# Spreading a weight conversion over two experts and moving token steps in a fused scan, mixture and gated-layer kernel

## The chip, the cores and the metric

The kernel runs on one core of a Trainium2 chip. The metric is device microseconds of one execution; before the change the median of three runs is 889.12 us (888.71 to 890.1). One more execution was profiled: it took 889.29 us, and its span from the first to the last instruction is 887.6 us. PE is the matrix engine (TensorE), DVE the vector engine, ACT the scalar engine, POOL is GpSimd, and SP issues the DMAs. Times inside the profile are microseconds from the start of the span.

## The reference, cut to what matters

Three layers follow each other on 3072 tokens of width 256. The first is a decayed scan over 4 sequences of 8 heads. Its result goes through four weighted experts, and their sum through a gated layer:

```python
x = scan(x, a, B, C)                       # (3072, 256)
p = domain_probs / (domain_probs.sum(-1, keepdims=True) + 1e-09)
out = 0
for e in range(4):                         # w1[e]: 256 x 1024, w2[e]: 1024 x 256
    h = np.maximum(x @ w1[e], 0.0)
    out += p[:, e:e + 1] * (h @ w2[e])
g = out @ w_gate                           # 256 x 1536
silu = g * (1.0 / (1.0 + np.exp(-g)))
val = out @ w_val
return silu * val @ w_out                  # 1536 x 256
```

The weights of the gated layer (called the dense layer below) are handed to the kernel as 64-bit numbers, which it turns into 32-bit ones itself.

## The kernel before, in words

Each operand of a matrix product is split into a high part (rounded to the matrix engine's fp32r) and a low part (the rest), and each product is three matmuls: high by high, low by high, high by low. A matmul takes 128 x 128 weights against 512 tokens.

The program text sets the order on every engine; the engines run in order and wait for one another by semaphores. The text has three stages:

- Scan together with experts 0 and 1, up to about 327 us.
- Experts 2 and 3. A unit is (expert, block of 512 tokens, chunk of 128 hidden columns): 2 x 6 x 8 = 96 units. `m_hidden` multiplies into a PSUM bank; ACT makes the high part `hh` (L551), DVE the low part `hl` (L552). `m_out`, three units later (LAG = 3), multiplies by the second weights into `po`. At the end of a block DVE multiplies by the token's probability (`tmp`, L572) and adds into `acc` (L574). Each unit has two slots at which other work is written in, so there are 192 slots.
- The dense layer in 18 quads: 3 pairs of token blocks by 6 quads of hidden columns. A quad has two halves: the gate (`what` = 0) and the value (`what` = 1). A half is seven products, after a scheme with seven instead of eight block products, in four PSUM banks X, Y, Z, W. The first four open the banks (A11, S2, S1, S3), then `rest` adds three more onto X, Z and W. ACT copies X to `c1` (tile `c`) before the fifth product may add onto X; DVE adds it up to `u` and `v`. In the gate's half ACT applies the silu to four results `s` (one straight from X, three after a DVE addition); in the value's half DVE multiplies the values with them, ACT makes the high part `ah` (L830) and POOL the low part `al` (L832). The two parts of four results (keys 22, 11, 12, 21) are multiplied by the output weights one quad later, in `dense_project`, between the products. The last quad's low parts are all made by DVE.

Two kinds of preparation run beside this. `dense_chunk` converts the dense weights in nine chunks (gate, value and output for each of three groups of columns). A chunk has two loads, two runs of nine DVE steps (L624 to L644), for gate and value four sums on POOL (`ws`, L658), then high parts on ACT (`wd_h`, L673), low parts on POOL (`wd_l`, L675) and two stores to DRAM. Chunks 3 to 8 are stored only and loaded again; chunks 0 to 2 also stay resident for the first pair. `dense_steps` strings the steps of several chunks into one list, and `spread` puts the list evenly over a range of the 192 slots. Before, the six chunks 3 to 8 lie in slots 18 to 96 and the three chunks 0 to 2 in slots 102 to 188 (n1 = 96 is where expert 3 begins).

`dense_tokens` prepares a pair of token blocks for the seven-product scheme in six steps s0 to s5: high parts on ACT (`xh`, `t3h`, `t24h`, L732), low parts and differences on POOL (L735, L738). For the first pair the steps lie in expert 3's slots 136 to 178, as they do after the change. For the other pairs they were written behind a quad: s0 and s1 behind the first quad of the pair before, s2, s3, s4 and s5 behind the second to fifth.

Of the kernel before, what the change touches and what calls it, by code (L numbers as in the profile page):

```python
# [16 lines left out]
def kernel(ctx: ExitStack, tc: tile.TileContext, nat_d, bc_d, bc0_d, a_d, probs, w1, w2, wg, wv, wo, out):  # L17
# [12 lines left out]
    nc = tc.nc  # L30
# [9 lines left out]
    KD = DM // P  # L40
    FC1 = F1 // P
# [6 lines left out]
    LAG = 3  # L48
# [21 lines left out]
    bxh = [xpool.tile([P, KD, BN], F32R, name=f"xh{i}", tag=f"xh{i}") for i in range(NBLK)]  # L70
    bxl = [xpool.tile([P, KD, BN], F32R, name=f"xl{i}", tag=f"xl{i}") for i in range(NBLK)]
    bacc = [xpool.tile([P, KD, BN], F32, name=f"acc{i}", tag=f"acc{i}") for i in range(NBLK)]
# [264 lines left out]
    def a_diff(q):  # L337
        L = Q[q]["L"]
        nc.vector.tensor_tensor(out=L, in0=L, in1=cols(cum, q).unsqueeze(2).to_broadcast([P, H, P]), op=ALU.subtract)
# [187 lines left out]
    def bank(pool, tag):  # L527
        return pool.tile([P, 512], F32, tag=tag, name=tag)
# [162 lines left out]
    def dense_steps(chunks):  # L691


        parts = [dense_chunk(*c) for c in chunks]
        seq = list(parts[0][0])
        stores = []
        for i, (_, halves, splits, own) in enumerate(parts):
            ahead = parts[i + 1][0] if i + 1 < len(parts) else [None, None]
            for z in range(2):
                seq += halves[z]  # L700
                if ahead[z]:
                    seq.append(ahead[z])
                if z == 0:
                    seq += stores
            seq += splits
            stores = own
        return seq + [lambda: None] * 8 + stores
# [17 lines left out]
    xt = {}  # L725

    def dense_tokens(p):

        b1, b2 = 2 * p, 2 * p + 1
        G = nc.gpsimd  # L730
        def high(out, raw):
            nc.scalar.activation(out=out, in_=raw, func=AF.Copy)  # L732

        def low(out, raw, hi):
            G.tensor_tensor(out=out, in0=raw, in1=hi.bitcast(F32), op=ALU.subtract)  # L735

        def sub(out, a, b):
            G.tensor_tensor(out=out, in0=a, in1=b, op=ALU.subtract)  # L738

        def s0():  # L740
            high(bxh[b1], bacc[b1])
            high(bxh[b2][:, 1, :], bacc[b2][:, 1, :])
            low(bxl[b2][:, 1, :], bacc[b2][:, 1, :], bxh[b2][:, 1, :])

        def s1():

            sub(bacc[b2][:, 1, :], bacc[b2][:, 1, :], bacc[b2][:, 0, :])
            low(bxl[b1], bacc[b1], bxh[b1])

        def s2():  # L750

            sub(bacc[b2][:, 0, :], bacc[b2][:, 0, :], bacc[b1][:, 0, :])
            G.tensor_tensor(out=bacc[b1][:, 0, :], in0=bacc[b2][:, 1, :], in1=bacc[b1][:, 0, :], op=ALU.add)

        def s3():

            sub(bacc[b1][:, 1, :], bacc[b1][:, 1, :], bacc[b1][:, 0, :])
            xt[p, "t3"] = [dpools["xt"].tile([P, BN], F32R, tag=f"t3{z}", name=f"t3{z}", bufs=2) for z in "hl"]
            high(xt[p, "t3"][0], bacc[b2][:, 1, :])
            high(bxh[b2][:, 0, :], bacc[b2][:, 0, :])  # L760
            low(bxl[b2][:, 0, :], bacc[b2][:, 0, :], bxh[b2][:, 0, :])

        def s4():
            xt[p, "t24"] = [dpools["xt"].tile([P, KD, BN], F32R, tag="xt", name=f"t24{z}") for z in "hl"]
            high(xt[p, "t24"][0], bacc[b1])
            low(xt[p, "t3"][1], bacc[b2][:, 1, :], xt[p, "t3"][0])

        def s5():
            low(xt[p, "t24"][1], bacc[b1], xt[p, "t24"][0])

        return [s0, s1, s2, s3, s4, s5]


    A11, A22, A12, S1, S2, S3, S4 = range(7)

    def operand(p, name):
        b1, b2 = 2 * p, 2 * p + 1
        if name == "T3":
            return xt[p, "t3"]
        v, k = {  # L780
            "B11": ((bxh[b1], bxl[b1]), 0),
            "B21": ((bxh[b1], bxl[b1]), 1),
            "B22": ((bxh[b2], bxl[b2]), 1),
            "T1": ((bxh[b2], bxl[b2]), 0),
            "T2": (xt.get((p, "t24")), 0),
            "T4": (xt.get((p, "t24")), 1),
        }[name]
        return [z[:, k, :] for z in v]

    def product(ps, w, a, v, start):  # L790
        ws = slice(a * P, (a + 1) * P)
        (wh, wl), (vh, vl) = w, v
        for i, (x, y) in enumerate([(wh, vh), (wl, vh), (wh, vl)]):
            nc.tensor.matmul(ps, x[:, ws], y, start=(start and i == 0), stop=(i == 2), skip_group_check=True)  # L794

    def temp(tag):
        if tag in ("c1", "u"):
            return mpool.tile([P, BN], F32, tag="ma" if tag == "c1" else "mb", name=tag)
        return dpools["dt"].tile([P, BN], F32, tag=tag, name=tag, bufs=5 if tag == "s" else 1)

    def dense_hidden(p, q, what, s):

        w = wq.pop((p, q, what))
        X, Y, Z, W = (bank(*b) for b in (banks[0], banks[1], banks[2], banks[3]))
        V = nc.vector
        put = lambda ps, a, v, start: product(ps, w, a, operand(p, v), start)
        c1, u, v = temp("c1"), temp("u"), temp("v")
        put(X, A11, "B11", True)
        nc.scalar.activation(out=c1, in_=X, func=AF.Copy)
        put(Y, S2, "T2", True)  # L810
        V.tensor_tensor(out=u, in0=Y, in1=c1, op=ALU.add)  # L811
        put(Z, S1, "T1", True)
        V.tensor_tensor(out=v, in0=Z, in1=u, op=ALU.add)  # L813
        put(W, S3, "T3", True)

        def out(key, ps, add, dst):

            if what == 0:
                s[key] = temp("s")
                if add is not None:  # L820
                    V.tensor_tensor(out=s[key], in0=ps, in1=add, op=ALU.add)  # L821
                nc.scalar.activation(out=s[key], in_=ps if add is None else s[key], func=AF.Silu)  # L822
                return
            if add is not None:
                V.tensor_tensor(out=dst, in0=ps, in1=add, op=ALU.add)
            av = s.pop(key)
            V.tensor_tensor(out=av, in0=ps if add is None else dst, in1=av, op=ALU.mult)  # L827
            ah = hpool.tile([P, 512], F32R, tag="hh", name="ah")
            al = hpool.tile([P, 512], F32R, tag="hl", name="al")
            nc.scalar.activation(out=ah, in_=av, func=AF.Copy)  # L830
            low = V if (p, q) == quads[-1] else nc.gpsimd
            low.tensor_tensor(out=al, in0=av, in1=ah.bitcast(F32), op=ALU.subtract)  # L832
            hid[p, q, key] = ah, al

        out(22, W, v, v)

        def rest():
            put(X, A12, "B21", False)
            out(11, X, None, None)
            put(Z, S4, "B22", False)  # L840
            out(12, Z, u, v)
            put(W, A22, "T4", False)
            out(21, W, u, u)
        return rest
# [27 lines left out]
    with tc.manual_schedule():  # L872
# [20 lines left out]
        def add(u, half, fn):  # L893
            todo.setdefault((u, half), []).append(fn)
# [5 lines left out]
        for q in range(NFIRST, NQ):  # L900
            for o, fn in points(q).items():
                if q == NFIRST and o < -4:
                    fn = {-7: lambda: a_diff(2), -6: lambda: a_causal(2)}.get(o)
                elif q == NFIRST and o == -4:
                    fn = lambda: a_weigh_b(2, nc.gpsimd)
# [27 lines left out]
        def spread(seq, slots):  # L933
            for i, fn in enumerate(seq):
                add(*slots[i * len(slots) // len(seq)], fn)
# [2 lines left out]
        add((2, 0, 0), 0, opens)  # L938
        slots = [(u, h) for u in units23 for h in range(2)]
        n1 = len(slots) // 2  # L940
        spread(dense_steps([(c, False) for c in (3, 4, 5, 6, 7, 8)]), slots[2 * (8 + LAG) - 4:n1])
        spread(dense_steps([(c, True) for c in (0, 1, 2)]), slots[n1 + 2 * LAG:-4])
        n2 = n1 + 2 * (2 * FC1 + LAG) + 2
        spread(dense_tokens(0), slots[n2:n2 + 42])

# [12 lines left out]
        quads = [(p, q) for p in range(NPAIR) for q in range(NQD)]  # L958
        AHEAD = 2
        dtodo = {}  # L960
# [7 lines left out]
        def project_part(i):  # L968
            if before:
                dense_project(*before, parts[i], outw[before])  # L970
            elif i < 2:
                for u in units[-LAG:-1] if i == 0 else units[-1:]:
                    m_out(u)
# [3 lines left out]
        for i, (p, q) in enumerate(quads):  # L977
            if i + AHEAD < len(quads):
                dense_load(*quads[i + AHEAD])
            outw[p, q] = wq.pop((p, q, 2))  # L980
            s = {}
            for what in range(2):
                rest = dense_hidden(p, q, what, s)
                project_part(2 * what)
                rest()
                project_part(2 * what + 1)
            for fn in dtodo.pop((p, q), []):
                fn()
            before = p, q
        for i in range(4):  # L990
            project_part(i)
# [53 lines left out]
```

## Time and profile before

| what | value |
| --- | --- |
| median of three runs | 889.12 us (888.71 to 890.1) |
| the profiled execution | 889.29 us, span 887.6 us |
| PE busy | 865.8 us, 98% of the span |
| DVE, ACT, POOL busy | 577.6, 343.8, 323.0 us |
| mean granted clock of PE | 0.989 |

Shares of the whole span hide the stages. The views to read are PE's timeline (when does a matmul start later than the pace of its neighbours), the table by windows, what the late ones waited for, and the chain of waits.

### The profile page before, as it was taken

The page shows a single profiled execution, that of the slowest core. Times are in us where ns is not written, and L with a number is a line of the kernel's source. Part 1 is how long each engine was busy: PE and PEld are TensorE (multiplying, and loading weights), DVE is VectorE, ACT ScalarE, POOL GpSimd, SP SyncE. Part 2 cuts the span into 40 slices and gives each one's busy share as a digit, 9 for nine tenths or more (in the row PEclk, how much of TensorE's full clock was granted, in tenths as well). Part 3 has the DMA queues.
Part 4 walks back from the last instruction along what each step waited for, and adds up shares of the span by engine and source line. Part 5 has one row for each costly group of instructions (what it writes and reads, how often), then busy time and mean ns, then how long its engine had stood idle before and what let it go on. Part 6 is the DMA issues. An engine that isn't in the chain of part 4 may idle for free.

```text
span 887.6 us, 12199 instructions
## 1 busy us (share of the span) xinstructions
PE 865.8 (98%) x4484; PEld 713.0 (80%) x4484; DVE 577.6 (65%) x884; ACT 343.8 (39%) x598; POOL 323.0 (36%) x276
## 2 busy tenths in 40 slices
PE   9999999999999999999899999998999999999997
PEld 8888888888888888887678888886877877788885
DVE  6877566656654443789776666736666766667675
ACT  5555444444343332222222233224344443444432
POOL 6755333323331121331330154204464374625250
PEclk8999999999999999999999999999999999999999
DMA  7844433343250132144352223034344264537301
GB/s 219 284 144 138 137 113 114 119 134 116 94 163 13 38 114 63 60 142 164 135 199 83 72 108 127 23 134 161 128 141 156 92 245 141 172 107 261 107 1 47
DMA packets 45523, 111.12 MB, mean 125 GB/s; under 512 B 5016, under 2 KB 12376, under 8 KB 45464
## 3 DMA queue, kind: packets, MB, share of 16 engines
q1 hardware_dynamic: 45464, 110.35, 36.8%
q8 instruction: 35, 0.57, 0.2%
q14 instruction: 24, 0.20, 0.1%
HBM read 92.88 MB, written 17.45 MB: 124 GB/s over the span
## 4 chain that ended last, share of the span: by engine, by line
PE 78%; DVE 11%; ACT 3%; issue 3%; POOL 2%; DMA 1%; SPq 0%; ACTq 0%; DVEq 0%; POOLq 0%
PE h L508 21%; PE po L516 18%; PE h L794 12%; PE po L861 5%; PE d L794 5%; PE d L516 5%; PE d L861 4%; PE d L508 2%; DVE hl L552 2%; PE ypsum L437 1%; POOL ws L658 1%; PE scores L391 1%; PE ypsum L400 1%; DVE dr L630 1%; DVE dr L634 1%
## 5 line engine op out<-in xcount | busy, mean ns | idle before, releaser
L552 DVE SCALAR_TENSOR_TENSOR hl<-h,hh 128x512 fp32r<-128x512 f32 (+1 forms) x184 | 117.9, 642 | 175.8 <-ACT hh L551 175.7
L551 ACT ACTIVATE hh<-h 128x512 fp32r<-128x512 f32 (+1 forms) x184 | 102.0, 560 | 267.5 <-PE h L508 267.5
L832 POOL TENSOR_TENSOR al<-s,ah 128x512 fp32r<-128x512 f32 x68 | 100.5, 1507 | 157.0 <-ACT ah L830 142.3
L508 PE MATMUL h<-xh,w_h 128*128 128x512 f32 (+1 forms) x368 | 139.0, 378 | 0.6 <-DVE hl L552 0.4
L508 PE MATMUL h<-xl,w_h 128*128 128x512 f32 (+1 forms) x368 | 137.5, 374 | 0.5 <-DVE xl L476 0.5
L508 PE MATMUL h<-xh,w_l 128*128 128x512 f32 (+1 forms) x368 | 137.0, 372 | 0.4 <-POOL w_l L125 0.4
L516 PE MATMUL po<-hh,w_l 128*128 128x512 f32 (+1 forms) x320 | 118.0, 369 | 2.1 <-POOL w_l L125 2.1
L516 PE MATMUL po<-hl,w_h 128*128 128x512 f32 (+1 forms) x320 | 118.1, 369 | 1.5 <-DVE hl L552 1.5
L516 PE MATMUL po<-hh,w_h 128*128 128x512 f32 (+1 forms) x320 | 118.5, 370 | 1.1 <-ACT L L349 0.6
L830 ACT ACTIVATE ah<-s 128x512 fp32r<-128x512 f32 x72 | 45.3, 632 | 101.8 <-DVE s L827 86.5
L508 PEld LDWEIGHTS h<-xh,w_h 128*128 128x128 f32 x368 | 69.4, 189 | 16.2 <-issue 3.6
L508 PEld LDWEIGHTS h<-xl,w_h 128*128 128x128 f32 x368 | 69.5, 189 | 14.5 <-DVE xl L476 2.6
L508 PEld LDWEIGHTS h<-xh,w_l 128*128 128x128 f32 x368 | 69.4, 189 | 11.9 <-POOL w_l L125 0.6
L516 PEld LDWEIGHTS po<-hl,w_h 128*128 128x128 f32 x320 | 60.3, 188 | 12.4 <-DVE hl L552 2.3
L516 PEld LDWEIGHTS po<-hh,w_h 128*128 128x128 f32 x320 | 60.3, 188 | 12.0 <-issue 1.3
L516 PEld LDWEIGHTS po<-hh,w_l 128*128 128x128 f32 x320 | 60.2, 188 | 12.0 <-POOL w_l L125 2.3
L811 DVE TENSOR_TENSOR u<-h,c 128x512 f32<-128x512 f32 x36 | 24.9, 692 | 62.0 <-PE h L794 36.4
L358 POOL TENSOR_TENSOR Bs<-bc,Bs 64x512 fp32r<-64x512 f32 x22 | 31.3, 1421 | 81.4 <-issue 72.0
L794 PE MATMUL h<-xh,wq_h 128*128 128x512 f32 x128 | 50.5, 394 | 2.1 <-DVE v L813 2.0
L822 ACT ACTIVATE s<-s 128x512 f32<-128x512 f32 x54 | 34.1, 631 | 46.0 <-DVE s L821 45.3
L658 POOL TENSOR_TENSOR ws<-dr 128x256 f32<-128x256 f32 x12 | 9.0, 753 | 114.4 <-DVE dr L644 114.4
L794 PE MATMUL h<-xl,wq_h 128*128 128x512 f32 x128 | 49.8, 389 | 0.0
(221 smaller groups left out, 1775.4 us busy)
## 6 DMA issues: line engine op xcount, KB each, us to landing
wq_h<-wd_d SPq DMA_DIRECT2D x32, 448.0 KB
wq_l<-wd_d SPq DMA_DIRECT2D x32, 448.0 KB
bc<-in_bc_dram SPq DMA_DIRECT2D x22, 512.0 KB
L<-crow_d SPq DMA_DIRECT2D x22, 512.0 KB
wq_o<-wo_d SPq DMA_DIRECT2D x16, 512.0 KB
nat<-in_nat_dram SPq DMA_DIRECT2D x24, 256.0 KB
raw<-in_w_dram SPq DMA_DIRECT2D x11, 512.0 KB
pbc<-probs_d SPq DMA_DIRECT2D x22, 256.0 KB
```

Of the source, the lines that this page charges most:

```text
L358: nc.gpsimd.tensor_tensor(out=r["Bs"][64:], in0=r["Br"][64:], in1=r["Bs"][64:].bitcast(F32), op=ALU.subtract)
L508: nc.tensor.matmul(ps, w[:, k, fs], v[:, k, :], start=(i == 0), stop=(i == len(ops) - 1))
L516: nc.tensor.matmul(po[d], w[:, fc, dsl], x, start=(first and i == 0), stop=(last and i == 2))
L551: nc.scalar.activation(out=hh, in_=ph, func=AF.Relu)
L552: nc.vector.scalar_tensor_tensor(out=hl, in0=ph, scalar=0.0, in1=hh.bitcast(F32), op0=ALU.max, op1=ALU.subtract)
L658: nc.gpsimd.tensor_tensor(out=v[:, :, o, :], in0=a, in1=b, op=op)
L794: nc.tensor.matmul(ps, x[:, ws], y, start=(start and i == 0), stop=(i == 2), skip_group_check=True)
L811: V.tensor_tensor(out=u, in0=Y, in1=c1, op=ALU.add)
L822: nc.scalar.activation(out=s[key], in_=ps if add is None else s[key], func=AF.Silu)
L830: nc.scalar.activation(out=ah, in_=av, func=AF.Copy)
L832: low.tensor_tensor(out=al, in0=av, in1=ah.bitcast(F32), op=ALU.subtract)
L861: nc.tensor.matmul(po[d], x[:, dsl], y, start=(first and i == 0), stop=(last and i == 2))
```

## The change

Three edits. The nine chunks' steps are spread anew: chunks 3 to 8 over slots 8 to 128 and chunks 0 to 2 over slots 128 to 188. The token steps of the next pair are written behind the gate's first four products of the same quads, no longer behind the quad; two high parts of 1024 columns are split in two of 512. In the last quad the low parts of keys 22 and 11 go to POOL; those of 12 and 21 stay on DVE.

```diff
         def s0():
-            high(bxh[b1], bacc[b1])
+            for k in range(KD):
+                high(bxh[b1][:, k, :], bacc[b1][:, k, :])
             high(bxh[b2][:, 1, :], bacc[b2][:, 1, :])
             low(bxl[b2][:, 1, :], bacc[b2][:, 1, :], bxh[b2][:, 1, :])
...
         def s4():
             xt[p, "t24"] = [dpools["xt"].tile([P, KD, BN], F32R, tag="xt", name=f"t24{z}") for z in "hl"]
-            high(xt[p, "t24"][0], bacc[b1])
+            for k in range(KD):
+                high(xt[p, "t24"][0][:, k, :], bacc[b1][:, k, :])
             low(xt[p, "t3"][1], bacc[b2][:, 1, :], xt[p, "t3"][0])
...
-            low = V if (p, q) == quads[-1] else nc.gpsimd
+            low = V if (p, q) == quads[-1] and key in (12, 21) else nc.gpsimd
             low.tensor_tensor(out=al, in0=av, in1=ah.bitcast(F32), op=ALU.subtract)
...
-        spread(dense_steps([(c, False) for c in (3, 4, 5, 6, 7, 8)]), slots[2 * (8 + LAG) - 4:n1])
-        spread(dense_steps([(c, True) for c in (0, 1, 2)]), slots[n1 + 2 * LAG:-4])
+        cut = n1 + 4 * FC1
+        spread(dense_steps([(c, False) for c in (3, 4, 5, 6, 7, 8)]), slots[FC1:cut])
+        spread(dense_steps([(c, True) for c in (0, 1, 2)]), slots[cut:-4])
...
                 rest = dense_hidden(p, q, what, s)
+                if what == 0:
+                    for fn in dtodo.pop((p, q), []):
+                        fn()
                 project_part(2 * what)
                 rest()
                 project_part(2 * what + 1)
-            for fn in dtodo.pop((p, q), []):
-                fn()
             before = p, q
```

How the instructions stand on the engines, at three places. On DVE in expert 2, one run of nine conversion steps of chunk 4 (tile f) among the low parts hl of the units; before:

```order
L552 SCALAR_TENSOR_TENSOR hl<-d_3793,hh 128x512
L624 TENSOR_SCALAR dr<-f_3715 128x2x256
L626 TENSOR_SCALAR dr<-dr 128x2x256
L628 TENSOR_SCALAR dr<-dr 128x2x256
L552 SCALAR_TENSOR_TENSOR hl<-h_3820,hh 128x512
L630 SCALAR_TENSOR_TENSOR dr<-f_3715,dr 128x2x256
L632 TENSOR_SCALAR f_3715<-f_3715 128x512
L634 TENSOR_TENSOR dr<-dr,f_3715 128x2x256
L636 TENSOR_SCALAR f_3715<-f_3715 128x512
L552 SCALAR_TENSOR_TENSOR hl<-h_3841,hh 128x512
```

and now, the same run of steps:

```order
L552 SCALAR_TENSOR_TENSOR hl<-h_3784,hh 128x512
L626 TENSOR_SCALAR dr<-dr 128x2x256
L628 TENSOR_SCALAR dr<-dr 128x2x256
L630 SCALAR_TENSOR_TENSOR dr<-f_3650,dr 128x2x256
L552 SCALAR_TENSOR_TENSOR hl<-d_3804,hh 128x512
L632 TENSOR_SCALAR f_3650<-f_3650 128x512
L634 TENSOR_TENSOR dr<-dr,f_3650 128x2x256
L636 TENSOR_SCALAR f_3650<-f_3650 128x512
L552 SCALAR_TENSOR_TENSOR hl<-h_3824,hh 128x512
```

There were three or four steps between two units, now there are two or three. On ACT at the first quads of the dense layer (xh is a token step's high part, c the copy of X, s the silu, ah the high part of a product); before:

```order
L822 ACT_TABLE_LOAD
L822 ACTIVATE s<-s 128x512
L822 ACTIVATE s<-h_5643 128x512
L822 ACTIVATE s<-s 128x512 x2
L809 ACTIVATE c_5713<-h_5709 128x512
L830 ACTIVATE ah<-s 128x512 x4
L732 ACTIVATE xh_80<-acc_92 128x1024
L732 ACTIVATE xh_81<-acc_93 128x512
L809 ACTIVATE c_5782<-h_5778 128x512
```

and now:

```order
L824 ACT_TABLE_LOAD
L824 ACTIVATE s<-s 128x512
L732 ACTIVATE xh_80<-acc_92 128x512 x2
L732 ACTIVATE xh_81<-acc_93 128x512
L824 ACTIVATE s<-h_5645 128x512
L824 ACTIVATE s<-s 128x512 x2
L811 ACTIVATE c_5721<-h_5717 128x512
L832 ACTIVATE ah<-s 128x512 x4
L811 ACTIVATE c_5785<-h_5781 128x512
```

The high parts moved from ahead of the next quad's c to ahead of the silu that reads X. On DVE in the last quad's value half (al is the low part); before:

```order
L825 TENSOR_TENSOR v<-d_7962,v 128x512
L827 TENSOR_TENSOR s<-v,s 128x512
L832 TENSOR_TENSOR al<-s,ah 128x512
L827 TENSOR_TENSOR s<-h_7959,s 128x512
L832 TENSOR_TENSOR al<-s,ah 128x512
L825 TENSOR_TENSOR v<-h_7961,u 128x512
L827 TENSOR_TENSOR s<-v,s 128x512
L832 TENSOR_TENSOR al<-s,ah 128x512
L825 TENSOR_TENSOR u<-d_7962,u 128x512
L827 TENSOR_TENSOR s<-u,s 128x512
L832 TENSOR_TENSOR al<-s,ah 128x512
```

and now:

```order
L827 TENSOR_TENSOR v<-d_7968,v 128x512
L829 TENSOR_TENSOR s<-v,s 128x512
L829 TENSOR_TENSOR s<-h_7965,s 128x512
L827 TENSOR_TENSOR v<-h_7967,u 128x512
L829 TENSOR_TENSOR s<-v,s 128x512
L834 TENSOR_TENSOR al<-s,ah 128x512
L827 TENSOR_TENSOR u<-d_7968,u 128x512
L829 TENSOR_TENSOR s<-u,s 128x512
L834 TENSOR_TENSOR al<-s,ah 128x512
```

The first two low parts left DVE; they stand at the end of POOL's line. The order on PE is the same as before.

## Rows read from the trace of the kernel before

**Rows 1.** The page: busy time, share of the span, instructions.

```profile
PE 865.8 (98%) x4484; PEld 713.0 (80%) x4484; DVE 577.6 (65%) x884; ACT 343.8 (39%) x598; POOL 323.0 (36%) x276
```

**Rows 2.** Timeline of PE: start, duration, instruction; the first matmuls of three units.

```profile
327.12 0.39 PE L508 MATMUL h<-xh,w_h 128*128 128x512 f32 x1
...
329.84 0.39 PE L508 MATMUL h<-xh,w_h 128*128 128x512 f32 x1
...
594.76 0.39 PE L508 MATMUL d<-xh,w_h 128*128 128x512 f32 x1
```

**Rows 3.** Windows of experts 2 and 3: stretch, its length, busy time by engine.

```profile
core 0: us, PE busy (x) PEld busy (x) DVE busy (x) ACT busy (x) POOL busy (x), PEclk, DMA share, GB/s
327.00:352.00 25.00, 25.00 (x112) 20.71 (x111) 10.05 (x15) 7.79 (x12) 4.81 (x2) 1.00 0.23 74
...
396.00:466.00 70.00, 64.17 (x269) 50.89 (x268) 59.32 (x102) 18.90 (x36) 22.18 (x22) 0.98 0.46 158
466.00:510.00 44.00, 44.00 (x196) 36.42 (x195) 26.78 (x49) 11.19 (x20) 4.17 (x5) 1.00 0.25 78
510.00:578.00 68.00, 68.00 (x302) 56.31 (x301) 48.88 (x74) 22.67 (x40) 28.19 (x22) 1.00 0.24 86
```

**Rows 4.** Timeline of four engines in expert 2; in brackets idle time and releaser.

```profile
331.52 9.70 SPq L607 DMA_DIRECT2D f<-in_wg_dram  x2
...
345.63 0.69 DVE L552 SCALAR_TENSOR_TENSOR hl<-h,hh 128x512 fp32r<-128x512 f32 x1 [2.03 <-ACT hh L551]
...
353.42 0.39 PE L516 MATMUL d<-hl,w_h 128*128 128x512 f32 x1
...
373.21 0.63 ACT L673 ACTIVATE wd_h<-ws 128x512 fp32r<-128x512 f32 x1 [2.50 <-POOL ws L658]
...
437.70 0.50 PE L516 MATMUL d<-hl,w_h 128*128 128x512 f32 x1 [3.14 <-DVE hl L552]
...
439.18 0.63 PE L508 MATMUL d<-xh,w_l 128*128 128x512 f32 x1
```

**Rows 5.** Chain of waits, dense stage: start, length, engine, tile and line.

```profile
597.64 2.04 PE h L794 x9
...
606.48 2.04 PE h L794 x9
...
624.33 2.04 PE h L794 x9
...
639.28 2.04 PE h L794 x9
...
868.35 1.38 PE h L794 x6
881.12 1.93 PE po L861 x6
```

**Rows 6.** Instructions of tile f, one line: duration in ns, least/median/most.

```profile
L630 DVE SCALAR_TENSOR_TENSOR dr<-f,dr x18: 675/693/1665, 357.6 to 568.4; 128x512 int32<-128x512 int32 x18
```

**Rows 7.** Timeline of ACT and PE around token steps, and one silu without them.

```profile
616.23 1.56 ACT L732 ACTIVATE xh<-acc 128x1024 fp32r<-128x1024 f32 x2
617.70 0.57 ACT L809 ACTIVATE c<-h 128x512 f32<-128x512 f32 x1
...
618.33 0.50 PE L794 MATMUL h<-xh,wd_h 128*128 128x512 f32 x1 [1.36 <-ACT c L809]
...
637.25 0.58 ACT L822 ACTIVATE s<-h 128x512 f32<-128x512 f32 x1
```

**Rows 8.** Last low parts on POOL, DVE, PE's wait; a group by lines (mean ns).

```profile
863.34 1.29 POOL L832 TENSOR_TENSOR al<-s,ah 128x512 fp32r<-128x512 f32 x1
...
873.53 0.69 DVE L832 TENSOR_TENSOR al<-s,ah 128x512 fp32r<-128x512 f32 x1 [0.70 <-ACT ah L830]
...
881.12 0.73 PE L861 MATMUL po<-ah,wq_o 128*128 128x512 f32 x2 [0.87 <-ACT ah L830]
...
L827 DVE TENSOR_TENSOR s<-u,s 128x512 f32<-128x512 f32 x18 | 18.1, 1007 | 0.6
```

## The prediction

> **What bounds the kernel now.** The page comes first: TensorE (PE) is busy for 98% of the span [rows 1]. Only the time in which PE waits or runs slowly can be gained, so I looked for it stage by stage.
>
> The timeline of PE gives the steady pace: two neighbouring units of experts 2 and 3 start 2.72 us apart, that is 12 matmuls of 0.2267 us. From the first of these 96 units to the last it takes 594.76 - 327.12 = 267.64 us; 95 units at the steady pace take 258.40. So 9.24 us are lost there [rows 2]. The table of windows says where. PE is full in 327 to 352, in 466 to 510 and in 510 to 578, and has 64.17 of 70 us in 396 to 466. There DVE is at 85%, against 40% ahead of the dense weights' conversion [rows 3]. The reader is to see that the loss lies in the stretch where DVE is fullest. The waits say how: PE stands for hl, DVE's low part of a hidden unit, 3.14 us at 437.70, and soon afterwards a matmul takes 0.63 us where 0.39 is usual [rows 4], with a granted clock below 1 in that window: some of the loss is the slow clock (1.2 instead of 2.4 GHz) that follows the standing.
>
> The chain of waits gives the dense stage. A half of a quad is 33 matmuls, 7.48 us. From 624.33 to 868.35 there are 32 halves, 239.36 us; it took 244.02, so 4.66 are lost. The first two quads are short of projections: 39 matmuls (8.84 us, as shown, 597.64 to 606.48), then 21 + 33 = 54, which should take 12.24 and took 17.85: 5.61 lost. From 868.35 to the end of the last six matmuls there are 57, 12.92 us; they ended at 881.12 + 1.93 = 883.05, 1.78 late [rows 5]. All four: 9.24 + 5.61 + 4.66 + 1.78 = 21.29 us. Without any of it the profiled execution (889.29 us, span 887.6) would take 868.0. That is the floor of this change, since it removes no matmul.
>
> **The weights' conversion, spread anew.** The 96 units are 192 slots of 1.36 us. Before, six chunks lie in slots 18 to 96 (13 a chunk) and three in 102 to 188 (28.7 a chunk). Afterwards each of the nine has 20 slots. What a chunk costs DVE comes from the windows: (26.78 + 48.88) / 112 = 67.6% in expert 3, less the 40.2% without conversion, is 27.4% at 28.7 slots a chunk, so 10.7 us a chunk [rows 3]. At 13 slots that is 60%, with the base 101%: DVE cannot keep up, and this is the stretch that stalls. At 20 slots it is 39%, with the base 80%, in both experts. PE forgives much: in the quiet stretch a low part ends at 346.32 and is first read at 353.42, 7.1 us later [rows 4]. A block's end (four more DVE operations) or a burst of steps takes less than that, and 20% spare gives it back.
>
> What else moves with the steps: their loads and stores on SP, the sums and low parts on POOL, the high parts on ACT. The first two loads were issued between 331.52 and 341.22 [rows 4]; the first step now comes at slot 9, about 327.12 + 9 x 1.36 = 339.4, 8 us after the first load, and the second half's at slot 17 (350.2). If it were not there, DVE would stand with hl behind it, covered by the 7.1 us. ACT stands behind POOL's sums at each chunk (2.50 us at 373.21 [rows 4]) with the next hh behind it; that also stays under 7.1 us. In expert 3 POOL has the first pair's token steps besides. Bounds: at worst, half of a chunk's 18 steps meet POOL as the worst step of its line did, 1.665 us against 0.675 [rows 6]: 9 x 0.99 = 8.9 us more per 27.3 us, DVE at 112%, 60 slots (82 us) give 9.8 us too much, less the 7.1 of cover, 2.7 us of stall. At best nothing is left. So the gain lies between 6.5 and 9.2; I take 8.9, since expert 3 shows PE full already at 68%.
>
> **The token steps moved into the gate's half.** Before, the next pair's high parts stand on ACT between the last ah of a quad and c, the copy that the fifth product of the next quad's first half waits for. At 616.23 two of them take 1.56 us, c follows at 617.70, and PE, after 1.36 us of waiting, goes on at 618.33 [rows 7]. Now they stand behind the first silu of the gate's half, where ACT has room: what follows them is the silu that reads bank X, at 637.25 in a quad without steps. X is needed by the value half at 639.28 [rows 5]. Each high part of 512 columns is 1.56 / 3 = 0.52. Two of them (the steps of the third and fourth quad of a pair) move that silu to 638.3, done by 638.9: no wait. Three (the first quad) move it to 638.8, done at 639.4: 0.1 to 0.3 us of wait. On POOL the steps come before the quad's own low parts. The most is the first quad's, four times 512 columns at 1.29 [rows 8] = 5.2 us from 638.8 on. The next low part is due after four products, two DVE operations and an ah, 639.28 + 2.7 + 1.4 + 0.6 = 644.0: no cost, if barely.
>
> The 4.66 us of the 32 halves are five such places (two for pair 1, three for pair 2); all but 0.3 goes, gain 4.3. It is less at the sixth, the 5.61 us of the first two quads. The product that waits for c is due 39 matmuls after 606.48, at 615.32, and starts at 618.33, 3.0 late: 1.36 is its wait, 1.65 were lost before, with DVE behind because of the last expert's sums, and 2.6 are lost after it. The 1.65 stay, and POOL's new work next to these sums may add 0.6. Without the high parts c starts at 616.23 and ends at 616.8; the next products then wait for v, two DVE operations of 0.7 later, 0.9 us in all. That leaves 3.2, and the gain is 2.4; the bounds are 0.7 (half of the 1.36) and 4.0 (all but the 1.65).
>
> **The tail.** In the last quad DVE makes a low part only after ACT's high part: it stands 0.70 us and works 0.69 [rows 8], four times. Two go to POOL, so DVE's line ahead of the last ah becomes 2 x 1.39 = 2.8 us shorter; PE's wait for it is 0.87 us [rows 8], with some small ones ahead of it. POOL takes 1.29 for such a part [rows 8]: the first from 873.53 to 874.8, the second to about 876.1. PE reads them from 876.3 and 877.6 on (868.35 plus 33 and 39 matmuls, and two more). So PE becomes its own bound, and 1.7 of the 1.78 us go. POOL beside DVE is not free: a product of two SBUF operands that runs beside POOL's low parts takes 1.007 us [rows 8], 0.32 more than the 0.69 of a low part without POOL, which also has two. The 2.8 us carry that.
> The Trainium skill (SBUF — State Buffer, section "Who interferes with whom") says that a DVE instruction with two SBUF inputs and a GpSimd instruction that reads SBUF shut each other out for a whole instruction. The row shows 0.32 and not 1.29 more on the mean. By the rule DVE would be a whole low part later, and the tail's gain would be about 1.4 instead of 1.7.
>
> **Sum.** 8.9 + 4.3 + 2.4 + 1.7 = 17.3. From the profiled execution's 889.29 that gives 872.0; the median of the runs lies 0.17 lower, so 871.8.
>
> **Rivals.**
> 1. Expert 3 takes over the stall. It gets 20 slots a chunk where it had 28.7, beside the token steps on POOL. For it: PE stalled in the stretch where DVE was at 85%, and 80% is close. Against it: 72% in 510 to 578, tokens included, with PE full [rows 3]. Price: 2.7 us by the bound above to half of the old 9.24: 875 to 876.5.
> 2. The token steps only move their wait: the silu behind them frees X late, and the value half starts late at all six places. For it: ACT executes in order and only 2 us lie between 637.25 and 639.28. Against it: two high parts need 1.04. Price: the 6.7 us of gain are lost, 878.5.
> 3. Slower than before: DVE falls behind for good in expert 3, every step held by POOL as in the worst row. Then 18 x 0.99 = 17.8 us come on top of each chunk, three chunks are 53 us, less the 16 us spare (20% of 82) and 7.1 of cover: 30 us of stall in place of the 9.24 that go. That is 889.1 + 30 - 8.9 - 8.4 = about 902. It decides from the point where some 80% of the steps are held so long. Against it: the product beside POOL in rows 8 loses 0.32 on the mean, not 0.99.
> 4. The spread does not do what it should: stalls in expert 2 come from ACT standing behind POOL's sums and not from DVE's load. Then half of 9.24 stays, 876.5. Against it: these sums also run in expert 3, where PE is full.
>
> **How the numbers follow.** My forecast 871.8 has 70%; rival 1 has 11%, rival 2 has 7%, rival 4 has 6%, rival 3 has 3%, and 3% is for mishaps that cancel the gain. Within the forecast the parts' bounds give 869.5 (everything but 1.5 us goes) to 875. The range reaches to rivals 1, 4 and most of 2: 869.5 to 878. A measurement of this kernel can tell 0.2%, 1.8 us, from no change: faster 0.94, the same 0.02, slower 0.04.
>
> **What would show it.** Right: PE full in every window from 327 to 597 with DVE near 80% in both experts; unit starts 267.6 us apart before, at most 259.5 now; halves of 7.48 us at the token steps; PE without a wait for ah in the last quad; a granted clock of 1.00 in experts 2 and 3. Wrong: PE waiting for hl in expert 3 (rival 1 or 3); PE waiting for a silu at the start of value halves (rival 2); the first two quads losing over 5 us still; PE waiting for POOL's al at the end.

## The result and the profile after

The changed kernel takes 875.46 us (median of five runs, 874.4 to 877.0) against 889.13 (888.71 to 890.1) before: ratio 0.984, 95% interval 0.983 to 0.986. The forecast was 871.8, the range 869.5 to 878.0. So it is faster by 13.7 us, inside the range and 3.7 slower than forecast. The profiled execution took 876.32 us with a span of 874.6. In two of the experiments below one execution ran at a low granted clock (0.65, the profiled one of its run, and 0.85); the times and ratios given there leave it out.

The page's busy line answers to [rows 1]; PE has the same instructions and is busy 4.9 us less:

```profile
PE 860.9 (98%) x4484; PEld 713.5 (82%) x4484; DVE 582.4 (67%) x882; ACT 344.1 (39%) x604; POOL 326.9 (37%) x278
```

The timeline of PE (start, duration, instruction; in brackets idle time and releaser), with the first matmuls of the first and the last of the 96 units, answers to [rows 2]; between them stands the one place where PE is late:

```profile
328.27 0.39 PE L508 MATMUL h<-xh,w_h 128*128 128x512 f32 x1
...
564.25 0.50 PE L516 MATMUL d<-hl,w_h 128*128 128x512 f32 x1
...
587.07 0.39 PE L508 MATMUL d<-xh,w_h 128*128 128x512 f32 x1
```

587.07 - 328.27 = 258.80 us, 0.40 over the steady 258.40, where it was 9.24. The windows of the same stretch answer to [rows 3] (columns as there): PE is full in all but one, the granted clock is 1.00 in all, and DVE has 69, 75, 73 and 76%, where the windows shown in [rows 3] have 40, 85, 61 and 72:

```profile
353.00:397.00 44.00, 44.00 (x196) 36.44 (x195) 30.38 (x53) 13.32 (x24) 15.21 (x16) 1.00 0.28 97
397.00:457.00 60.00, 60.00 (x266) 49.69 (x265) 44.94 (x79) 16.08 (x28) 10.06 (x10) 1.00 0.30 100
457.00:500.00 43.00, 43.00 (x191) 35.62 (x190) 31.46 (x51) 12.37 (x22) 11.23 (x10) 1.00 0.44 154
500.00:568.00 68.00, 67.91 (x300) 55.90 (x299) 51.45 (x79) 22.36 (x40) 30.67 (x25) 1.00 0.32 109
```

The chain of waits answers to [rows 5] (the first products of the dense stage, of the second and the third quad and of the last half, and the last six matmuls):

```profile
589.95 2.04 PE h L796 x9
...
606.96 3.59 PE h L796 x9
...
616.41 2.04 PE h L796 x9
...
857.21 2.04 PE h L796 x9
868.77 1.40 PE po L863 x6
```

The stage's pieces, before and after, worked out as in the prediction:

| piece | lost before | lost after | gain | forecast |
|---|---|---|---|---|
| 96 units of experts 2 and 3 | 9.24 | 0.40 | 8.84 | 8.9 |
| first two quads (589.95 to 616.41: 26.46; before 26.69) | 5.61 | 5.38 | 0.23 | 2.4 |
| 32 halves (616.41 to 857.21: 240.80; steady 239.36) | 4.66 | 1.44 | 3.2 | 4.3 |
| tail (857.21 to 870.17: 12.96; steady 12.92) | 1.78 | 0.04 | 1.74 | 1.7 |

That is 14.0 us. The two profiled executions differ by 12.97: expert 2 starts 1.15 us later in the one of after (328.27 against 327.12), before anything that the change touches; the profiled executions of the experiments, whose code is the same up to there, start it at 326 to 330.

The miss sits in the first two quads. The timeline of DVE, POOL and PE there, with the last expert's output sums (acc), u and v, and the product that waits for them (x2 merges two instructions; the second acc is shown again by itself):

```profile
597.37 1.30 POOL L735 TENSOR_TENSOR xl<-acc,xh 128x512 fp32r<-128x512 f32 x1 [18.59 <-ACT xh L732]
598.15 1.37 DVE L572 TENSOR_TENSOR tmp<-po,pbc 128x512 f32<-128x512 f32 x2
598.75 1.29 POOL L738 TENSOR_TENSOR acc<-acc 128x512 f32<-128x512 f32 x1
599.43 3.95 DVE L574 TENSOR_TENSOR acc<-acc,tmp 128x512 f32<-128x512 f32 x2
600.01 2.83 POOL L735 TENSOR_TENSOR xl<-acc,xh 128x1024 fp32r<-128x1024 f32 x1
...
600.52 2.87 DVE L574 TENSOR_TENSOR acc<-acc,tmp 128x512 f32<-128x512 f32 x1
...
603.31 0.68 DVE L813 TENSOR_TENSOR u<-h,c 128x512 f32<-128x512 f32 x1
...
604.84 0.50 PE L796 MATMUL h<-xh,wd_h 128*128 128x512 f32 x1 [2.65 <-DVE v L815]
```

The reader is to see ends, not lengths. The second sum (600.52 + 2.87 = 603.39) ends 0.55 after POOL's long low part (600.01 + 2.83 = 602.84); the first (599.43 + 1.16) ends 0.55 after POOL's subtraction (600.04). So each sum did its work only when POOL's instruction was all but over. That holds beyond this place: of the DVE operations of 128x512 with both operands in SBUF (`acc`, the products `s`, `al`) that start inside an instruction of POOL after 327 us, 35 of 35 in the kernel before and 40 of 42 in the changed one end 0.54 to 0.58 after it, and the other two met only its first 0.01 or last 0.03 us. The two tmp ahead of them read a bank of PSUM and one SBUF operand; they run in 0.69 each, beside POOL.

In the halves, the second largest wait left is the one that rival 2 spoke of, in the second pair's first quad. ACT has three high parts, then the silu that frees bank X:

```profile
689.85 1.66 ACT L732 ACTIVATE xh<-acc 128x512 fp32r<-128x512 f32 x3
...
691.41 0.58 ACT L824 ACTIVATE s<-h 128x512 f32<-128x512 f32 x1
...
692.04 0.50 PE L796 MATMUL h<-xh,wq_h 128*128 128x512 f32 x1 [0.19 <-ACT s L824]
```

### The profile page after: what moved, and what is told of

It reads as the page before. It is cut to its first block, busy times and chain, and to the rows that moved or that the text cites. A ratio compares the mean times of both kernels' runs of the same rounds, so it can differ in the third digit from the quotient of the medians.

```text
span 874.6 us, 12212 instructions
## 1 busy us (share of the span) xinstructions
PE 860.9 (98%) x4484; PEld 713.5 (82%) x4484; DVE 582.4 (67%) x882; ACT 344.1 (39%) x604; POOL 326.9 (37%) x278
## 4 chain that ended last, share of the span: by engine, by line
PE 87%; DVE 5%; POOL 2%; issue 2%; DMA 2%; ACT 1%; SPq 0%; POOLq 0%; ACTq 0%; DVEq 0%
PE h L508 24%; PE po L516 21%; PE h L796 14%; PE d L516 6%; PE d L863 6%; PE po L863 5%; PE d L796 5%; PE d L508 3%; DMA raw<-in_w_dram 2%; PE ypsum L437 1%; PE scores L391 1%; PE ypsum L400 1%; DVE hl L552 1%; POOL ws L658 1%; POOL w_l L125 1%
## 5 line engine op out<-in xcount | busy, mean ns | idle before, releaser
L834 POOL TENSOR_TENSOR al<-s,ah 128x512 fp32r<-128x512 f32 x70 | 103.5, 1509 | 129.8 <-ACT ah L832 111.7
L824 ACT ACTIVATE s<-s 128x512 f32<-128x512 f32 x54 | 33.4, 629 | 43.0 <-DVE s L823 42.2
L796 PE MATMUL h<-xh,wq_l 128*128 128x512 f32 x128 | 49.8, 389 | 0.0
```

## The experiments

All times are medians of their runs; ratios are against runs of the kernel before on the same chip (889.12, 890.3 and 888.97 us in the three sets). The first set does one part of the change at a time, on the kernel before.

**The spread alone.**

```diff
-        spread(dense_steps([(c, False) for c in (3, 4, 5, 6, 7, 8)]), slots[2 * (8 + LAG) - 4:n1])
-        spread(dense_steps([(c, True) for c in (0, 1, 2)]), slots[n1 + 2 * LAG:-4])
+        cut = n1 + 4 * FC1
+        spread(dense_steps([(c, False) for c in (3, 4, 5, 6, 7, 8)]), slots[FC1:cut])
+        spread(dense_steps([(c, True) for c in (0, 1, 2)]), slots[cut:-4])
```

> The kernel before with the new spread of the conversion alone (slots 8 to 128 and 128 to 188). Theory: DVE's load of 101% in expert 2 was the cause, and the three edits add up. In the changed kernel's profile the 96 units lost 0.40 us against 9.24, so this kernel gains 8.8: 880.3 us (879.5 to 881.3), with PE full from 327 to 597. Rival (the edits don't add up; expert 3's new load costs more when the token steps behind it stand as before): 882 to 885.

879.19 us, ratio 0.989 (0.988 to 0.991): 9.9 us, of which the units' 8.8 can be seen in its trace; one stall is left there, the same 0.36 us as in the changed kernel. Another 1.3 are in the first two quads, which lose 4.27 here against 5.61: the matmuls at half speed that the profile of before has there (620.44 to 623.0) are missing in this one. One matmul, before and here:

```profile
620.87 0.63 PE L794 MATMUL h<-xl,wd_h 128*128 128x512 f32 x1
...
611.19 0.40 PE L794 MATMUL h<-xl,wd_h 128*128 128x512 f32 x1
```

The 32 halves lose 4.93 (4.66 before) and the tail what it lost before.

**The token steps alone.**

```diff
                 rest = dense_hidden(p, q, what, s)
+                if what == 0:
+                    for fn in dtodo.pop((p, q), []):
+                        fn()
...
-            for fn in dtodo.pop((p, q), []):
-                fn()
```

> The kernel before with the token steps in the gate's half alone. Theory: the five places of pair 1's and 2's other steps gain 3.2 us (4.66 to 1.44), the first two quads next to nothing (5.61 to 5.4), because POOL's three operations in the first quad hold up DVE's two additions into acc: 889.1 - 3.4 = 885.7 us (885.0 to 886.5). Rival (the move costs nothing in the first quad and the miss lies elsewhere): 882.5.

886.2 us, ratio 0.996 (0.995 to 0.998). By the pieces of the table the first two quads lose 5.42 us, as in the changed kernel (5.38), with the two sums at 3.95 us again; the 32 halves lose 0.85 instead of 4.66.

**The tail alone.**

```diff
-            low = V if (p, q) == quads[-1] else nc.gpsimd
+            low = V if (p, q) == quads[-1] and key in (12, 21) else nc.gpsimd
```

> The kernel before with two of the last quad's low parts on POOL alone. Theory: PE is its own bound from there on, 1.7 us less: 887.4 us (886.9 to 887.9). Rival (by POOL's lock on DVE only half of it): 888.2.

886.73 us, ratio 0.998 (0.996 to 0.999); no wait is left in its last quad. The three parts alone give 9.9 + 2.9 + 2.4 = 15.2, together 13.7: each came out within 1.1 us of what was expected here, the spread and the tail below the stated range. The 1.5 that the sum is too large is about the 1.3 that the spread alone gains in the first two quads and the changed kernel does not keep. The forecast's miss is inside a part: the token steps gave 2.9 by themselves, and the prediction had 6.7 for them.

**Pair 1's token steps one quad later.** From here on the edits are on the changed kernel.

```diff
-            for i, fn in zip((0, 0, 1, 2, 3, 4), dense_tokens(p + 1)):
+            for i, fn in zip((1, 1, 2, 3, 4, 5) if p == 0 else (0, 0, 1, 2, 3, 4), dense_tokens(p + 1)):
```

> The changed kernel with pair 1's token steps one quad later each (s0 and s1 in the second quad's gate half, away from the last expert's additions into acc). Theory (lock: DVE's additions, two SBUF operands each, wait for whole POOL instructions): the two additions take 1.3 us again instead of 3.95, PE's wait of 2.65 at 604.84 and the slow clock behind it go; 1.65 us stay in the first quad, 0.9 in the second, 0.3 at X: the first two quads lose about 2.9 instead of 5.3, and the time is 873.0 us (872.3 to 873.8). Rival (ACT's three high parts ahead of the silu that reads X, or the table load, put the first quad late): the loss comes along into the second quad, 875.4.

872.87 us, ratio 0.982 (0.980 to 0.984). The two sums take 1.28 us again. This moves ACT's high parts as well as POOL's low parts, so the next one splits them.

**Only POOL's part one quad later**: ACT's high parts of s0 (three instructions) stay in the first quad, POOL's low part of s0 and the steps s1 to s5 of this pair come one quad later.

```diff
-            low(bxl[b2][:, 1, :], bacc[b2][:, 1, :], bxh[b2][:, 1, :])
+            if p != 1:
+                low(bxl[b2][:, 1, :], bacc[b2][:, 1, :], bxh[b2][:, 1, :])
         def s1():
+            if p == 1:
+                low(bxl[b2][:, 1, :], bacc[b2][:, 1, :], bxh[b2][:, 1, :])
...
-            for i, fn in zip((0, 0, 1, 2, 3, 4), dense_tokens(p + 1)):
+            for i, fn in zip((0, 1, 2, 3, 4, 5) if p == 0 else (0, 0, 1, 2, 3, 4), dense_tokens(p + 1)):
```

> The changed kernel; of pair 1's token steps the four high parts stay in the first quad on ACT, only GpSimd's four low parts go to the second quad. Lock theory (the two sums of the last expert take 3.95 instead of 1.28 us because GpSimd's low parts run beside them): the sums take 1.3 again, no slow clock in the first quads, these lose about 3.3 as in the run with all token steps one quad later, 872.4 to 873.0 us. Rival (it is the high parts on ACT or the new order of the first quad that cost): the first two quads lose 5.4 as in the changed kernel, 875.4 us.

873.18 us (870.58 to 874.08), ratio 0.981 (0.979 to 0.984): too wide to tell 873 from 875.4, and without a profile whose rows can be set beside the others. It was run again, unaltered, in a set with the changed kernel itself:

> The same kernel as the run in which only GpSimd's part of pair 1's steps goes to the second quad, once more for its profile. Lock theory: the two sums take 1.3 us, the three high parts stand on ACT in the first quad without a wait of PE behind them, the first two quads lose about 3.3 us, 872.4 to 873.5 us. Rival: the first two quads lose 5.4 us, 875.4 us.

> The changed kernel once more, on the same chip as these two, so that differences of 2 us can be read: 875.5 us by either theory.

872.85 us (872.74 to 873.94), ratio 0.982 (0.981 to 0.983), against 876.65 (875.54 to 877.14), ratio 0.986 (0.984 to 0.987), for the changed kernel on the same chip: 3.8 us apart, no run of one among those of the other. Timeline of DVE in the run without POOL's work, the same two sums:

```profile
598.98 1.28 DVE L574 TENSOR_TENSOR acc<-acc,tmp 128x512 f32<-128x512 f32 x2
...
600.18 0.68 DVE L816 TENSOR_TENSOR u<-h,c 128x512 f32<-128x512 f32 x1
```

The same three high parts stand on ACT (1.66 us) as in the changed kernel, and PE's loss in the first two quads is 2.80 us against 5.42 in the second run of the changed kernel. The difference, 2.62, agrees with the sums' 3.95 - 1.28 = 2.67. The rest of the 3.8 us is 0.4 in the halves and 1.0 by which expert 2 starts earlier in this profile, before anything differs.

**POOL's work put back**, with results that are overwritten later and one high part on ACT that it reads, into the version whose token steps come one quad later.

```diff
+                    if (p, q) == quads[0]:
+                        nc.scalar.activation(out=bxh[3][:, 1, :], in_=bacc[3][:, 1, :], func=AF.Copy)
+                        for v in (bxl[3][:, 1, :], bxl[3][:, 0, :]):
+                            nc.gpsimd.tensor_tensor(out=v, in0=bacc[3][:, 1, :], in1=bxh[3][:, 1, :].bitcast(F32), op=ALU.subtract)
+                        nc.gpsimd.tensor_tensor(out=bxl[2], in0=bacc[2], in1=bacc[2], op=ALU.subtract)
+                        nc.gpsimd.tensor_tensor(out=bxl[3][:, 0, :], in0=bacc[3][:, 1, :], in1=bacc[3][:, 1, :], op=ALU.subtract)
```

> The kernel with pair 1's token steps one quad later (872.87 us), and in the first quad, where the changed kernel has them, one high part on ACT and four subtractions on GpSimd whose results are overwritten later (512, 512, 1024 and 512 columns, about 6.7 us). ACT has two high parts fewer there than in the changed kernel. Lock theory: the two sums of the last expert take 3.5 to 5.2 in place of 1.28 us, PE waits 2 to 4 us for the v behind them and runs at half clock afterwards: 874.9 to 876.9 us. Rival (ACT's high parts or the order of the steps cost the first quad its gain): sums 1.3 us, 872.9 to 873.3 us.

874.87 us, ratio 0.984 (0.983 to 0.985), against 872.87 and 0.982 (0.980 to 0.984) without, on another chip: 2 us slower, at the lower edge of the expected 874.9 to 876.9. The intervals overlap, so the traces have to decide. Its timeline:

```profile
597.16 1.90 POOL L994 TENSOR_TENSOR xl<-acc 128x1024 fp32r<-128x1024 f32 x1
597.76 3.29 DVE L574 TENSOR_TENSOR acc<-acc,tmp 128x512 f32<-128x512 f32 x2
...
599.01 1.49 POOL L995 TENSOR_TENSOR xl<-acc 128x512 fp32r<-128x512 f32 x1
...
602.50 0.50 PE L796 MATMUL h<-xh,wd_h 128*128 128x512 f32 x1 [1.99 <-DVE v L815]
```

The sums lose 2.0 us and the first two quads 1.95 (5.28 against 3.33). The sums end at 601.05, 0.55 after POOL's last (600.50), as in the changed kernel. POOL's two subtractions beside the sums were shorter than planned (1.90 and 1.49 us, where 1.29 and 2.83 stand in the changed kernel), and the effect is smaller with them. One expected thing did not come: PE did not fall to half clock here, nor in the second run of the changed kernel. The same matmul in the first and in the second profile of the changed kernel (the granted clock of the stretch is 0.50 in the first and 1.00 in the second):

```profile
607.98 0.63 PE L796 MATMUL h<-xl,wd_h 128*128 128x512 f32 x1
...
608.07 0.40 PE L796 MATMUL h<-xl,wd_h 128*128 128x512 f32 x1
```

The first two quads lose 5.38 in the one and 5.42 in the other. So the half-speed matmuls at 607.55 to 609.26 of the first profile cost nothing in the end: where they are missing, PE waits for DVE instead (at 610.09 and 613.85).

**Fewer DVE steps in expert 2**, on the kernel before. For the six chunks three of nine steps a half are left out, so a part of the conversion is not computed.

```diff
-        halves = [[step(z, i) for i in range(9)] for z in range(2)]
+        halves = [[step(z, i) for i in range(9) if resident or i not in (1, 2, 5)] for z in range(2)]
```

> The kernel before; for the six chunks converted in expert 2 three of the nine steps a half (all on DVE) are left out, so part of the conversion is not computed; GpSimd's sums and low parts and ACT's high parts stay where they were. Load theory (DVE at 101% is what stalls expert 2): at about 40 + 37 = 77% the 96 units lose at most 1 of their 9.24 us, about 880.5 us. Rival 4 of the prediction (ACT standing behind GpSimd's sums stalls it): half of the loss stays, 884.5 us or more.

879.89 us, ratio 0.990 (0.987 to 0.993). No gap is left in PE's 96 units. The window that answers to the stalled one of [rows 3], and one of ACT's waits in it:

```profile
397.00:467.00 70.00, 70.00 (x311) 57.96 (x310) 48.06 (x81) 21.11 (x38) 21.92 (x20) 1.00 0.51 179
...
435.85 0.63 ACT L673 ACTIVATE wd_h<-ws 128x512 fp32r<-128x512 f32 x1 [2.50 <-POOL ws L658]
```

DVE at 69% instead of 85, PE 70.00 of 70, with POOL's work as before (21.92 us, 22.18 in [rows 3]) and ACT still 2.24 and 2.50 us behind its sums. So the stalls of expert 2 were DVE's load, and rival 4 falls for this stage. The lead of the low parts says the same: from the end of a low part to its first reading by PE lie 7.09 us in the quiet stretch, in the kernel before less than 1 us at 13 of the 96 units and 0.05 at the least, here never less than 4.17.

**The border two blocks later**, so that the three resident chunks get 14.7 slots each.

```diff
-        cut = n1 + 4 * FC1
+        cut = n1 + 6 * FC1
```

> The changed kernel with the border between the six and the three chunks moved two units' blocks later, so that the three resident chunks get 14.7 slots each in place of 20, all of it inside expert 3. Load theory (share of DVE decides, and GpSimd's work lengthens it there): DVE at 40 + 53 = 93% plus contention, stalls come back in expert 3: 877.5 to 881.5 us. Rival (7 us of cover carry a stretch of 88 slots' end): no new stall, 875.5 us.

879.08 us, ratio 0.988 (0.986 to 0.990), inside the 877.5 to 881.5 of the load theory. The window of the last chunks and PE's first two stalls in it:

```profile
545.00:589.00 44.00, 40.79 (x175) 32.12 (x174) 36.76 (x56) 13.63 (x26) 19.96 (x17) 1.00 0.38 132
```

```profile
566.87 0.63 ACT L673 ACTIVATE wd_h<-ws 128x512 fp32r<-128x512 f32 x1 [2.56 <-POOL ws L658]
567.41 0.58 ACT L551 ACTIVATE hh<-h 128x512 fp32r<-128x512 f32 x1
...
568.04 0.50 PE L516 MATMUL d<-hh,w_h 128*128 128x512 f32 x1 [1.12 <-ACT hh L551]
...
572.57 0.50 PE L516 MATMUL d<-hl,w_h 128*128 128x512 f32 x1 [0.77 <-DVE hl L552]
```

DVE has 84%, as in the stalled window of before (85%), and PE stalls four times; the 96 units lose 4.75 us. The first stall is ACT's, standing 2.56 us behind POOL's sums: rival 4's mechanism exists, but shows here, with DVE at 84%, and not in expert 2 of the six-step run, where ACT stands 2.50 us behind the sums with DVE at 69%.

**The best of these**: all token steps one quad later, at most two high parts ahead of the silu that frees X, the border one block earlier.

```diff
-            for k in range(KD):
+            for k in range(1 if late else KD):
                 high(bxh[b1][:, k, :], bacc[b1][:, k, :])
...
-            low(bxl[b1], bacc[b1], bxh[b1])
+            if late:
+                low(bxl[b1][:, 0, :], bacc[b1][:, 0, :], bxh[b1][:, 0, :])
+            else:
+                low(bxl[b1], bacc[b1], bxh[b1])
...
+            if late:
+                high(bxh[b1][:, 1, :], bacc[b1][:, 1, :])
+                low(bxl[b1][:, 1, :], bacc[b1][:, 1, :], bxh[b1][:, 1, :])
...
-        cut = n1 + 4 * FC1
+        cut = n1 + 3 * FC1
...
-            for i, fn in zip((0, 0, 1, 2, 3, 4), dense_tokens(p + 1)):
+            for i, fn in zip((1, 1, 2, 3, 4, 5), dense_tokens(p + 1, True)):
```

> The changed kernel with all token steps one quad later for both pairs (so that none runs beside the last expert's sums), pair by pair at most two high parts ahead of the silu that frees bank X, and the border of the chunks one block earlier, so that the resident three have more slots. Lock theory: 2.4 us come back in the first two quads, the 0.47 us wait for X goes, and perhaps the 0.36 us in expert 3: 871.5 to 872.5 us. Rival (these losses come from elsewhere): 875.4 us.

871.23 us (870.65 to 872.8), ratio 0.980 (0.978 to 0.982): faster than both kernels, and just below the expected range. By the pieces of the table PE loses 3.2 us (7.3 in the changed kernel): nothing in the 96 units, 0.33 in the halves with no wait for X, and 2.83 in the first two quads, as without POOL's work there. The three edits were not taken apart here.

## Why the prediction was right, and where it was not

The time lies inside the range, but not by the whole mechanism. Three of the four steps came in, in the main, as forecast. The first two quads did not, and 875.46 lies just above the 875 that the parts' own bounds allow: the range holds it because it was stretched to the rivals' prices. That this is also the price of rival 1 is chance, for expert 3 lost 0.36 us and not 2.7 or more.

**The spread (8.9 forecast, 8.84 measured).** The step holds, and the six-step run and the later border show it from both sides: PE stalls with DVE at 85 and 84%, and at 69 to 76% not at all or once for 0.36 us. The cost of a chunk was put too high: over 353 to 568 DVE has 158.23 of 215 us, 73.6%, so 33.4% of 27.2 us = 9.1 us a chunk, not 10.7, and 74% and not 80. Rival 1 came in small: one stall of 0.36 us in expert 3, with a low part of 128x1024 on POOL ahead of it. There the lead of the low parts, 7.09 us at rest, is down to 0.05, so 76% in a window is no safe distance. Timeline of DVE, POOL and PE there:

```profile
560.46 2.85 POOL L735 TENSOR_TENSOR t24l<-acc,t24h 128x1024 fp32r<-128x1024 f32 x1
560.97 2.63 DVE L626 TENSOR_SCALAR dr<-dr 128x512 int32<-128x512 int32 x1
...
563.52 0.68 DVE L552 SCALAR_TENSOR_TENSOR hl<-d,hh 128x512 fp32r<-128x512 f32 x1
```

The bound "as the worst step of its line did, 1.665" [rows 6] was no bound: this step took 2.63, and the worst of the line in [rows 6] now takes 2.77.

**The first two quads (2.4 forecast, 0.23 measured).** This is the step that failed: "POOL's new work next to these sums may add 0.6". It added 2.6, and the gain fell below the step's own bound of 0.7; the prediction's sign of being wrong, "the first two quads losing over 5 us still", came. The rest of that step was about right: without POOL's work there the two quads lose 2.80 us, where 1.65 + 0.9 = 2.55 were forecast. One premise was unsteady: of the 5.61 lost before, 1.3 were half-speed matmuls, which the profile of the spread alone (4.27) does not have; why the clock fell in one and not in the other stays open. The prediction does not say where the 0.6 comes from; it is about twice the 0.32 that its tail takes from a mean, 1.007 against 0.69 [rows 8]. That mean does not say how long DVE is shut out; it says how late in POOL's instruction DVE happened to arrive. One of the 18 products behind the mean, with the low part that it met (the kernel before):

```profile
613.38 1.73 POOL L832 TENSOR_TENSOR al<-s,ah 128x512 fp32r<-128x512 f32 x1
...
614.60 1.05 DVE L827 TENSOR_TENSOR s<-u,s 128x512 f32<-128x512 f32 x1
```

It starts 0.51 us ahead of POOL's end at 615.11 and ends 0.54 after it. The trace of before held the case itself, in expert 3 (timeline of POOL and DVE, the kernel before):

```profile
562.58 2.40 POOL L735 TENSOR_TENSOR t24l<-acc,t24h 128x1024 fp32r<-128x1024 f32 x1 [6.49 <-ACT t24h L732]
563.39 2.74 DVE L574 TENSOR_TENSOR acc<-acc,tmp 128x512 f32<-128x512 f32 x2
```

The first of these two sums takes 2.14 us and ends at 565.53, 0.55 after POOL's 564.98. Priced by that row, sums that start inside POOL's run end 0.55 after its last instruction beside them, as they do in the changed kernel. The prediction cites the Trainium skill's rule for this (SBUF — State Buffer, section "Who interferes with whom"): two such instructions shut each other out for a whole instruction. It set the rule aside for the mean, and the trace agrees with the rule. Operations with one operand in PSUM and one in SBUF, as tmp, hl, u and v, stay at 0.69 at most beside POOL.

**The token places in the halves (4.3 forecast, 3.2 measured).** The waits for c went as forecast. Three places are left: 0.58 at 643.66, 0.47 at 692.04, 0.23 at 704.74. The second is the forecast's "0.1 to 0.3" behind three high parts, 0.2 more than worked out, and it goes when at most two stand there (the best version, where the steps also come one quad later). That is rival 2 at one place of six.

**The tail (1.7 forecast, 1.74 measured).** As forecast: POOL makes two low parts, and PE no longer waits. The prediction's other estimate, 1.4 by the rule, did not come: DVE's operations arrived near the ends of POOL's and were held for a fraction of a low part:

```profile
862.48 3.00 POOL L834 TENSOR_TENSOR al<-s,ah 128x512 fp32r<-128x512 f32 x2 [9.01 <-ACT ah L832]
...
863.41 0.92 DVE L829 TENSOR_TENSOR s<-v,s 128x512 f32<-128x512 f32 x1
...
865.09 0.94 DVE L834 TENSOR_TENSOR al<-s,ah 128x512 fp32r<-128x512 f32 x1 [0.76 <-ACT ah L832]
```

Each is 0.23 to 0.25 longer than 0.69, and the 2.8 us of relief carry it.

Of the 3.7 us between forecast and result, 2.2 are the first two quads and 1.1 the halves. The rest, 0.4, is no larger than what separates two executions ahead of expert 2, and stays open.

## What to carry to other kernels

Before work is moved to GpSimd, list the VectorE instructions with both operands in SBUF that will run beside it, and price each by the end of GpSimd's instruction, not by a mean over past collisions; long GpSimd instructions cost most. A stage stalls by the load of its own stretch: compare VectorE's share there (85% stalled, 76% lost 0.36 us) and not the average of the kernel, and look how far ahead of their readers its results are. When copies are put ahead of an activation that frees a bank, count them against the slack: two fitted here, three did not.

## What the runs showed of the hardware that was not expected

- An operation of VectorE with one SBUF input can be held too: the int32 TENSOR_SCALAR of 128x512 takes 0.43 us by the median and took 2.63 beside GpSimd's low part, ending 0.29 after it.
- The exclusion goes both ways: of the 70 low parts `al` of 128x512 on GpSimd in the changed kernel, the 33 that start while a product of two SBUF operands stands or runs on VectorE take 1.73 to 1.80 us and end 1.14 to 1.17 after it; the other 37 take 1.28 to 1.30.
- After PE's wait of 2.65 and 2.64 us at the same place, the clock fell to half in one profiled execution of the changed kernel and not in the other, and the first two quads lost 5.38 and 5.42 us.
